# Attention, matrix products and a routed layer in one kernel: where the first two chunks are normalised, and which banks two hash products use

## The chip, the cores and the metric

The kernel runs as one program on one core of a Trainium2 chip. The metric is device microseconds (us) of one execution, from three runs: 702.88 us median, 701.33 to 703.13. The profile shown here is one more execution of the same program, with its own time of 702.02 us.

## The reference

Three layers follow each other, all in float32. Only the order of the arithmetic matters here.

```python
# 1. attention with hash buckets (B=2, H=8, S=768, D=64)
q_bits = (einsum('bhsd,dk->bhsk', q, proj) > 0)      # 6 bits, the same for k
mask   = q_bucket[:, :, :, None] == k_bucket[:, :, None, :]
scores = where(mask, (1 / sqrt(64)) * q @ k.T, -1e9)
scores = scores - max(scores)
attn   = exp(scores) / (sum(exp(scores)) + 1e-9)
x      = attn @ v                                    # as (1536, 512)
# 2. x = ((x @ w1) * (x @ w2)) @ w3 @ w_out
# 3. one of 8 experts per token
logits = x @ w_gate + modality_bias[modality_id]
e      = argmax(logits)
out    = softmax(logits)[e] * (relu(x @ w1[e]) @ w2[e])
```

## The kernel before

**Attention in units.** A pair is two heads side by side in the 128 partitions; there are 8 pairs. A pair has 12 units in the first stage (6 blocks of 128 queries times 2 heads) and 12 in the second (2 halves of 384 queries times 6 blocks of 128 keys). A loop over `i` (the unit number, 0 to 107) writes one step of each stage after the other, by hand; nothing reorders them. In unit i the first stage works on unit i and the second on unit i-9.

- `stage_1` (line 316): TensorE multiplies one block of queries by all keys (tile `m`, two banks, line 326), and VectorE takes the maximum of each row (`TENSOR_REDUCE nm<-m`, line 333). After six units GpSimd prepares the maxima (lines 337 to 340), `stage_f` transposes them (`f`, line 344), ScalarE copies them out (`rT`, line 346), and a DMA puts them into two extra rows of the query tile, so that the second stage gets them subtracted for nothing.
- `stage_2` (line 354): TensorE computes the scores (`s`, line 361), ScalarE takes the exponential (`pt<-s`, line 362), and the block is added to the running sum (`acc`, line 368), on GpSimd, and in some units on VectorE. `m` and `s` share one ring of two buffers (`ps("s")`, four banks in all), so a late maximum or a late exponential holds up TensorE.
- `stage_a` (line 371): TensorE multiplies by the values (`a`, line 376).

**Work between the units.** `fill` takes pieces of weights from a queue: three VectorE operations (lines 493, 494, 483) rebuild a weight from 64-bit storage, until unit 85. From unit 86 on (`SWITCH`) the pieces are loaded again (`st<-wfd`) and split into a high part (ScalarE, line 474) and a low part (`w<-st,w`, VectorE, line 475), 16 of them, for the second layer. The w3-times-w_out product (`w`, line 553) fills TensorE up to unit 85.

**Normalisation.** The attention output of a batch lies unnormalised in `xT`, as 4 slabs `hp` of 128 rows. A chunk is 256 tokens; there are six. `load_r(ch)` (line 577) loads the reciprocals of the sums, spread over the partitions, into `rb`. `norm_x(ch, hp, part)` (line 583) has three parts: part 0 multiplies by `rb` and adds a correction `nw` (mean of the values, for rows whose sum is zero), part 1 copies the result to a float32r tile on ScalarE (`x<-xT`, line 594), part 2 writes the remainder on VectorE (line 596). `norm_step` (line 598) runs part 0 of one slab, part 1 of the slab before and part 2 of the one before that.

- Chunk 0: `load_r` in unit 88, `norm_step` in units 90 to 95. Its part 0 is `nw` on VectorE (line 590), the product on GpSimd (line 591) and the sum on VectorE (line 592).
- Chunk 1: `load_r` in unit 98, part 0 in units 101 to 104, all three operations on VectorE.
- From chunk 2 on, in the second layer, product and sum are on GpSimd.

**After it.** From unit 95 on `moe_half` (line 620) issues the first products of the second layer (`ab`, line 627) between the units; the first one needs all four slabs of chunk 0. From about 327 us on the second layer, the routing and the experts run.

**The start.** `hash_z` (line 239) computes the hash products of the pairs, `hash_bits` (line 251) turns them into bits on VectorE (`bt<-z`, line 258). For the second pair, which has nothing but the first pair ahead of it, the two halves are computed in units 1 and 2 into the banks with the tags `m` and `w`, and turned into bits in units 6 and 7. `stage_f` uses the bank `m` as well, in unit 6.

Of the kernel before, what the change touches and what calls it, by code (L numbers as in the profile page):

```python
# [13 lines left out]
ALU = mybir.AluOpType  # L14
# [4 lines left out]
B, H, S, D = 2, 8, 768, 64  # L19
NT, DM, DF, E = 1536, 512, 1024, 8  # L20
P = 128
HP = H // 2
# [9 lines left out]
CH = 256  # L32
# [6 lines left out]
SWITCH = 86  # L39
# [15 lines left out]
NSTEP = 4  # L55
PATTERN = (1, 1, 0, 1, 0)
HOOKS = (3, 24, 82)
RAWS = 4


def consts_array(proj):
# [95 lines left out]
def body(tc, qT, kT, vP, w1d, w2d, w3d, wod, mod, wgate, mbias, e1, e2, cst, out):  # L157
    nc = tc.nc
    PE, ACT, DVE, POOL, SP = nc.tensor, nc.scalar, nc.vector, nc.gpsimd, nc.sync
# [4 lines left out]
    def one(name, shape, dt=F32, at_top=False):  # L164
        n = 4
        for d in shape[1:]:
            n *= d
        rings[name] = Ring(mem, name, n, 1, at_top)
        return rings[name](shape, dt)

    def ring(name, words, n, at_top=False, below=None):
        return Ring(mem, name, 4 * words, n, at_top, below)
# [15 lines left out]
    def ps(tag, shape, name):  # L188
        return psum[0].tile(shape, F32, tag=tag, name=name, bufs=nbuf.get(tag, 1))
# [8 lines left out]
    mv = one("mv", [P, B, HP])  # L198
# [4 lines left out]
    wgp = one("wgp", [P, 8, 32])  # L203
    xT = {b: one(f"xT{b}", [P, HP, S + 1]) for b in range(B)}

    r_raw = ring("raw", S, 6, True)
    r_bt = ring("bt", S, 1, True)
    r_lo = ring("lo", S, 2, True)
    heads = {
        (nm, hd, i): one(f"{nm}{hd}{i}", [P, 2, S], F32R, True) for i in range(2) for nm in "qk" for hd in range(2)  # L210
    }
# [24 lines left out]
    def hash_half(pairs, half):  # L236
        hash_z(pairs, half)
        hash_bits(pairs, half)

    def hash_z(pairs, half, tag="m"):  # L240
        z = zs_t[half] = ps(tag, [P, HS], f"z{pairs[0]}{half}")
        for p in pairs:
            for j, nm in enumerate("qk"):
                r = 64 * (p % 2) + 32 * j
                PE.matmul(
                    z[r:r + 32, :], cs[:, 96 + 32 * j:128 + 32 * j], raw_t[p, nm][:, half * 384:half * 384 + 384],
                    start=True, stop=True, tile_position=(0, r),
                )

    def hash_bits(pairs, half):  # L250
        lo, hi = 64 * (pairs[0] % 2), 64 * (pairs[-1] % 2) + 64
        z = zs_t.pop(half)
        if half == 0:
            bt = r_bt([P, S], F32R)
            for p in pairs:
                bt_t[p] = bt
        bt = bt_t[pairs[0]]
        DVE.tensor_scalar(
            bt[lo:hi, half * HS:half * HS + HS], z[lo:hi, :], cs[lo:hi, 2:3], cs[lo:hi, 0:1], ALU.is_ge, ALU.mult)
# [173 lines left out]
    def piece_load(k):  # L433
        i = order[k]
        if k in raws:
            return
        if i < 8:
            src = wod[i * P:(i + 1) * P, :]
        elif i < 24:
            f, hf = divmod(i - 8, 2)  # L440
            src = w3d[f, :, hf * 4:hf * 4 + 4, :].rearrange("p g f -> p (g f)")
        else:
            m, j = divmod((i - 24) % 16, 8)
            c, hf = divmod(j, 2)
            src = ((w1d, w2d)[m] if i < 40 else wfd[m])[c * P:(c + 1) * P, hf * 512:hf * 512 + 512]
        if i < 40:
            raws[k] = r_cr([P, 1024])
            SP.dma_start(raws[k].bitcast(I64), src)
        else:
            raws[k] = r_st([P, 512])  # L450
            SP.dma_start(raws[k], src)
# [70 lines left out]
    def after(n, fn):  # L522
        todo_at.setdefault(slot[0] + n, []).append(fn)
# [47 lines left out]
                break  # L571


    rg, w34 = {}, []
    x_t, g_t, gf_t, lg_t, rb_t, xn_t = {}, {}, {}, {}, {}, {}

    def load_r(ch):
        rb_t[ch] = rg["rb"]([P, HP, CH])
        b, o = divmod(ch * CH, S)
        for j in range(2):  # L580
            SP.dma_start(rb_t[ch][64 * j:64 * j + 64], rd[b, j, :, o:o + CH].partition_broadcast(64))

    def norm_x(ch, hp, part):
        b, o = divmod(ch * CH, S)
        if part and ch not in x_t:
            x_t[ch] = rg["x"]([P, 2, HP, CH], F32R)
        x = xT[b][:, hp, o:o + CH]
        if part == 0:
            w = rg["nw"]([P, CH])
            DVE.tensor_scalar(w, rb_t[ch][:, hp, :], 0.0, mv[:, b, hp:hp + 1], ALU.is_lt, ALU.mult)  # L590
            (DVE if ch == 1 else POOL).tensor_mul(x, x, rb_t[ch][:, hp, :])
            (DVE if ch < 2 else POOL).tensor_add(x, x, w)
        elif part == 1:
            ACT.copy(x_t[ch][:, 0, hp, :], x)
        else:
            DVE.tensor_sub(x_t[ch][:, 1, hp, :], x, x_t[ch][:, 0, hp, :].bitcast(F32))

    def norm_step(ch, step):
        for hp, part in ((step - 2, 2), (step - 1, 1), (step, 0)):
            if 0 <= hp < HP:  # L600
                norm_x(ch, hp, part)

    TERMS = ((0, 0), (0, 1), (1, 0))
# [124 lines left out]
    for i in range(NU + LEAD + LAG + 2):  # L728
        slot[0] = i
        if i == SWITCH:  # L730
            assert done["n"] == 40 and done["w"] == len(w34q), done
            for r in (r_cr, r_T, r_ev, r_wT, r_w3, r_wo):
                r.close()
            w12 = [one(f"w{m}", [P, 2, 4, DF], F32R) for m in range(2)]
            r_st = ring("st", 512, 3)
            for m in (40, 41, 42):
                piece_load(m)
            for r in (r_raw, r_bt, r_lo):
                r.close()
            rg["x"] = ring("x", 2 * HP * CH, 1, True)  # L740
            rg["rb"] = ring("rb", HP * CH, 1, True)
            rg["nw"] = ring("nw", CH, 1, True)
            rg["gf"] = ring("gf", 4 * CH, 1, True)
            rg["asb"] = ring("asb", CH, 1, True)
        if i == 0:
# [8 lines left out]
        if i == 12:  # L754
            SP.dma_start(cs[:, 160:], cst[:, 160:])
            SP.dma_start(wgs[:, :, 0:E], wgate.rearrange("(c p) e -> p c e", p=P))
        if i == SWITCH + NSTEP - 2:
            load_r(0)
        if 0 <= i - SWITCH - NSTEP < HP + 2:
            norm_step(0, i - SWITCH - NSTEP)  # L760
        if i == 98:
            load_r(1)
        if 101 <= i < 101 + HP:
            norm_x(1, i - 101, 0)
        if i == NU - 12 + LEAD:
            for nm in "qk":
                for hd in range(2):
# [6 lines left out]
        p, ph = divmod(i, 12)  # L774
# [6 lines left out]
        if fi % 6 == 0 and 0 < fi <= NU and (i <= 6 or fi > 6):  # L781
            stage_f(*divmod(fi // 6 - 1, 2))
        if p == 0 and ph in (1, 2):
            hash_z([1], ph - 1, "mw"[ph - 1])
        elif p == 0 and ph in (6, 7):
            hash_bits([1], ph - 6)
        elif p % 2 == 1 and p + 1 < NPAIR and ph in (HASH, HASH + 1):
            hash_half([p + 1, p + 2], ph - HASH)
        for fn in todo_at.pop(i, []):
# [155 lines left out]
    for ch in range(NCH):  # L945
        if ch:
            g_t[ch] = rg["g"]([P, 2, 8, CH], F32R)
        for f in range(NEARLY if ch == 0 else 0, 8):
            if ch == 0:
                k = f - NEARLY  # L950
# [135 lines left out]
    r_eu = ring("eu", 2 * 4096, 2)  # L1086
    r_er = ring("er", 1024, RAWS)
    r_ex = ring("ex", 2 * 4 * G, 2)
# [29 lines left out]
    def more_loads(n=1):  # L1118
        for _ in range(n):
            if lq:  # L1120
                j, m, k = lq.pop(0)
                load_raw(j, m, k, eregs[j])
# [17 lines left out]

    more_loads(RAWS - PREA)

# [86 lines left out]
    held.clear()  # L1229
    more_loads(RAWS - PREL)  # L1230

# [231 lines left out]
```

## Time and profile before

| | |
|---|---|
| median of 3 runs | 702.88 us (701.33 to 703.13) |
| the profiled execution, time / span | 702.02 us / 700.2 us |
| TensorE matmul, busy | 662.9 us (95%) |
| VectorE, ScalarE, GpSimd, busy | 383.3, 315.1, 318.9 us (55%, 45%, 46%) |
| mean granted TensorE clock | 0.975 of full speed |
| DMA | 94.03 MB, 134 GB/s over the span |

PE is TensorE (PEld its weight loads), DVE VectorE, ACT ScalarE, POOL GpSimd, SP the engine that issues the DMAs. In the timeline a line is one group of like instructions that follow each other: start, summed duration, engine, line, what is written and read, and in square brackets how long the engine sat idle before it and what ended that wait. A granted clock of 1.00 is 2.4 GHz and 0.50 is 1.2 GHz. The span begins with the first instruction; some 2 us of the execution's time lie outside it.

### The profile page before, as it was taken

To read this page: it belongs to the slowest core of one execution; us is meant where nothing else is said; L and a number is where in the kernel's file an instruction comes from. 1 tells how busy PE (TensorE), PEld (TensorE's weight loads), DVE (VectorE), ACT (ScalarE), POOL (GpSimd) and SP (SyncE) were. 2 spreads that over 40 slices of the span, in tenths; PEclk is the share of its full clock that TensorE was granted. 3 is DMA by queue.
4 is the path that set the end of the run, shared out by engine and by line. 5 is a ranking of instruction groups with operands and counts; after the bars stand their busy time and mean duration, and the time that the engine had idled before them with its cause. 6 is when DMAs were issued, how large, how long until landed. Compare 5 with 4: busy or idle time off the path is not lost. (4 is left out here: it accounts for less than half of the span.)

```text
span 700.2 us, 10953 instructions
## 1 busy us (share of the span) xinstructions
PE 662.9 (95%) x4004; PEld 507.0 (72%) x4004; DVE 383.3 (55%) x613; ACT 315.1 (45%) x534; POOL 318.9 (46%) x316
## 2 busy tenths in 40 slices
PE   6888999999999998899999999999998999999995
PEld 2544665656565664567989898989887999899884
DVE  6897676658657657746451212121184765665550
ACT  7256554646545555353341212121213765565551
POOL 8499867677867677344351414050204132011110
PEclk9699999999999998799999999999999999999998
DMA  8757654363826442230401020100017887666530
GB/s 225 240 180 177 203 157 161 117 203 111 245 78 215 135 145 88 88 102 24 115 19 61 1 61 1 61 1 31 0 62 270 270 295 231 231 209 214 202 126 18
DMA packets 41691, 94.03 MB, mean 134 GB/s; under 512 B 6352, under 2 KB 12032, under 8 KB 41632
## 3 DMA queue, kind: packets, MB, share of 16 engines
q1 hardware_dynamic: 39552, 86.72, 39.2%
q0 software_dynamic: 2080, 6.56, 2.8%
q8 instruction: 33, 0.54, 0.3%
q14 instruction: 26, 0.21, 0.1%
HBM read 72.98 MB, written 12.94 MB: 123 GB/s over the span
## 5 line engine op out<-in xcount | busy, mean ns | idle before, releaser
L627 PEld LDWEIGHTS ab<-x,w 128*128 128x128 f32 x1152 | 139.9, 191 | 11.5 <-issue 4.4
L627 PE MATMUL ab<-x,w 128*128 128x256 f32 x1152 | 144.5, 285 | 1.5 <-ACT rT L346 0.9
L333 DVE TENSOR_REDUCE nm<-m 128x1 f32<-128x768 f32 x96 | 91.4, 955 | 73.6 <-PE m L326 73.1
L368 POOL TENSOR_TENSOR acc<-acc,pt 128x770 f32<-128x770 f32 x61 | 112.9, 1851 | 26.1 <-ACT pt L362 24.8
L362 ACT ACTIVATE pt<-s 128x768 f32<-128x768 f32 x96 | 77.9, 812 | 93.3 <-PE s L361 84.4
L361 PE MATMUL s<-q,k 128*128 128x384 f32 (+1 forms) x384 | 88.7, 355 | 8.7 <-DVE nm L333 7.1
L638 POOL TENSOR_TENSOR g<-gf,g 128x256 fp32r<-128x256 f32 x48 | 35.5, 739 | 127.8 <-ACT g L637 127.6
L361 PEld LDWEIGHTS s<-q,k 128*128 128x128 f32 (+1 forms) x384 | 70.9, 197 | 21.0 <-DVE nm L333 8.7
L376 PE MATMUL a<-pt,v 128*64 128x385 f32 x384 | 84.7, 521 | 0.0
L1130 DVE TENSOR_TENSOR eu<-er,eu 128x1024 fp32r<-128x1024 f32 x56 | 67.4, 1223 | 23.3 <-ACT eu L1129 22.4
L326 PEld LDWEIGHTS m<-k,q 78*128 78x128 f32 x192 | 30.9, 200 | 63.2 <-issue 20.1
L1318 POOL DMA_INDIRECT out<-o,sidx x13 | 14.1, 1088 | 124.6 <-ACT o L1317 107.9
L1292 PE MATMUL e1F<-ex,eu 128*128 128x256 f32 x576 | 70.3, 283 | 0.5 <-DVE ex L1258 0.3
L1292 PEld LDWEIGHTS e1F<-ex,eu 128*128 128x128 f32 x576 | 69.7, 190 | 1.4 <-DVE ex L1258 0.5
L636 DVE TENSOR_TENSOR gf<-asb,ab 128x256 f32<-128x256 f32 x48 | 20.2, 421 | 90.4 <-ACT asb L635 90.3
L1310 PE MATMUL e2F<-eu,h 128*128 128x512 f32 x288 | 68.8, 394 | 0.0
L326 PE MATMUL m<-k,q 78*128 78x384 f32 x192 | 61.8, 407 | 6.7 <-DVE nm L333 4.1
L1129 ACT CAST eu<-er 128x1024 fp32r<-128x1024 f32 x56 | 57.6, 1046 | 8.5 <-DMA er<-e 7.7
L1310 PEld LDWEIGHTS e2F<-eu,h 128*128 128x128 f32 x288 | 53.3, 188 | 11.1
L553 PE MATMUL w<-wo,w 128*128 128x512 f32 x192 | 58.2, 410 | 0.8 <-POOL w L475 0.8
L926 PE MATMUL x2p<-w,g 128*128 128x512 f32 x240 | 58.2, 397 | 0.0
L635 ACT COPY asb<-ab 128x256 f32<-128x256 f32 x48 | 17.9, 373 | 78.2 <-PE ab L627 78.2
(200 smaller groups left out, 790.5 us busy)
## 6 DMA issues: line engine op xcount, KB each, us to landing
er<-e SPq DMA_DIRECT2D x56, 512.0 KB
cr<-w3d SPq DMA_DIRECT2D x16, 512.0 KB
cr<-wod SPq DMA_DIRECT2D x8, 512.0 KB
cr<-w1d SPq DMA_DIRECT2D x8, 512.0 KB
wfd<-cT SPq DMA_DIRECT2D x16, 256.0 KB
cr<-w2d SPq DMA_DIRECT2D x8, 512.0 KB
st<-wfd SPq DMA_DIRECT2D x16, 256.0 KB
raw<-kT SPq DMA_DIRECT2D x8, 384.0 KB
```

What stands on the lines that cost most here:

```text
L326: PE.matmul(s[:, half, 0:HS], q[0:KROWS[hd], 0, qt * P:qt * P + P], k[0:KROWS[hd], 0, half * HS:half * HS + HS], start=True, stop=True,)
L333: DVE.tensor_reduce(nm[:, 3 * hd + qt % 3:3 * hd + qt % 3 + 1], s[:, :, 0:HS], AX.XY, ALU.max, negate=True)
L361: PE.matmul(s[:, hd, 0:HS], k[0:n, i, c * P:c * P + P], q[0:n, i, cl], start=(i == 0), stop=(i == 1))
L362: ACT.activation(pts[j % 4][:, :, 0:HS], s[:, :, 0:HS], AF.Exp, scale=SCALE)
L368: (DVE if on_dve else POOL).tensor_add(acc, pts[(j - 1) % 4] if c == 1 else acc, pts[j % 4])
L376: PE.matmul(a_t[p, half][64 * hd:64 * hd + 64, :], v[:, c, 64 * hd:64 * hd + 64], pts[j % 4][:, hd, :], start=(c == 0), stop=(c == QT - 1) ...
L553: PE.matmul(w34p[f], w3_t[f][:, st, g, :], wo[:, mv, g, :], start=(g == 0 and k == 0), stop=(g == 7 and k == 2))
L627: PE.matmul(ab[:, j, :], w12[j][:, st, c, fs], x[:, mv, c, :], start=(c == 0 and i == 0), stop=(c == 3 and i == 2))
L926: PE.matmul(st["ps"], g_t[ch][:, a, f, i * P:i * P + P], w34[b][:, f, :], start=(f == 0 and k == 0), stop=(f == 7 and k == 2),)
L1130: DVE.tensor_sub(t[:, 1, sl], raw, t[:, 0, sl].bitcast(F32))
L1292: PE.matmul(o[f], w[:, st, c, fs], x[:, mv, c, :], start=(c == 0 and i == 0), stop=(c == 3 and i == 2))
L1310: PE.matmul(o, h[:, st, f, sl], w[:, mv, f, :], start=(f == 0 and k == 0), stop=(f == 7 and k == 2))
```

## The change

Chunk 0 and chunk 1 get their reciprocals in units 74 and 90 (before: 88 and 98), and the twelve operations of part 0 of each are written one per unit, from unit 78 and from unit 94, all on VectorE, behind the unit's maximum and the queue's first operation. `norm_step` leaves part 0 out for these two chunks; parts 1 and 2 stay where they were. The rings `rb` and `nw` are taken at the start, and the ring `lo` loses its second buffer. The second pair's hash products go to the banks `u` and `w`, and the second half's bits are taken in unit 8.

```diff
+NORM = (74, 90)
...
+    rg = {"rb": ring("rb", HP * CH, 1, True), "nw": ring("nw", CH, 1, True)}
     r_raw = ring("raw", S, 6, True)
     r_bt = ring("bt", S, 1, True)
-    r_lo = ring("lo", S, 2, True)
+    r_lo = ring("lo", S, 1, True)
...
             DVE.tensor_scalar(w, rb_t[ch][:, hp, :], 0.0, mv[:, b, hp:hp + 1], ALU.is_lt, ALU.mult)
-            (DVE if ch == 1 else POOL).tensor_mul(x, x, rb_t[ch][:, hp, :])
-            (DVE if ch < 2 else POOL).tensor_add(x, x, w)
+            POOL.tensor_mul(x, x, rb_t[ch][:, hp, :])
+            POOL.tensor_add(x, x, w)
...
+    def norm_0(ch, hp, s):
+        b, o = divmod(ch * CH, S)
+        x = xT[b][:, hp, o:o + CH]
+        if s == 0:
+            DVE.tensor_mul(x, x, rb_t[ch][:, hp, :])
+        elif s == 1:
+            nw_t[ch, hp] = rg["nw"]([P, CH])
+            DVE.tensor_scalar(nw_t[ch, hp], rb_t[ch][:, hp, :], 0.0, mv[:, b, hp:hp + 1], ALU.is_lt, ALU.mult)
+        else:
+            DVE.tensor_add(x, x, nw_t.pop((ch, hp)))
+
     def norm_step(ch, step):
         for hp, part in ((step - 2, 2), (step - 1, 1), (step, 0)):
-            if 0 <= hp < HP:
+            if 0 <= hp < HP and (part or ch >= len(NORM)):
                 norm_x(ch, hp, part)
...
-        if i == SWITCH + NSTEP - 2:
-            load_r(0)
         if 0 <= i - SWITCH - NSTEP < HP + 2:
             norm_step(0, i - SWITCH - NSTEP)
-        if i == 98:
-            load_r(1)
-        if 101 <= i < 101 + HP:
-            norm_x(1, i - 101, 0)
+        for ch, at in enumerate(NORM):
+            if i == at and ch == 0:
+                load_r(0)
+            if i == at + 4:
+                for k in range(12):
+                    after(k, lambda ch=ch, k=k: norm_0(ch, k // 3, k % 3))
+            if i == at + 16 and ch + 1 < len(NORM):
+                load_r(ch + 1)
...
         if p == 0 and ph in (1, 2):
-            hash_z([1], ph - 1, "mw"[ph - 1])
-        elif p == 0 and ph in (6, 7):
-            hash_bits([1], ph - 6)
+            hash_z([1], ph - 1, "uw"[ph - 1])
+        elif p == 0 and ph in (6, 8):
+            hash_bits([1], ph // 2 - 3)
```

VectorE's order before, from the maximum of unit 89 to that of unit 92 (`m_2_1`, `m_3_0`, `m_3_1` and `m_4_0` are units 89 to 92):

```order
L333 TENSOR_REDUCE nm_2328<-m_2_1_2435 128x1
L368 TENSOR_TENSOR acc_2430<-acc_2430,pt_20_89 128x770
L475 TENSOR_TENSOR w_215_2368<-st_2370,w_215_2368 128x512
L590 TENSOR_SCALAR nw_2457<-rb_2414,mv_73 128x256
L592 TENSOR_TENSOR xT_10_79<-xT_10_79,nw_2457 128x256
L333 TENSOR_REDUCE nm_2464<-m_3_0_2461 128x1
L475 TENSOR_TENSOR w_216_2369<-st_2372,w_216_2369 128x512
L590 TENSOR_SCALAR nw_2481<-rb_2414,mv_73 128x256
L592 TENSOR_TENSOR xT_10_79<-xT_10_79,nw_2481 128x256
L333 TENSOR_REDUCE nm_2464<-m_3_1_2485 128x1
```

The same place in the changed kernel, whose line numbers are 2 higher here (lines 604, 607 and 609 are the three operations of `norm_0`):

```order
L335 TENSOR_REDUCE nm_2339<-m_2_1_2450 128x1
L609 TENSOR_TENSOR xT_10_79<-xT_10_79,nw_2434 128x256
L370 TENSOR_TENSOR acc_2445<-acc_2445,pt_20_89 128x770
L477 TENSOR_TENSOR w_219_2382<-st_2384,w_219_2382 128x512
L335 TENSOR_REDUCE nm_2479<-m_3_0_2476 128x1
L477 TENSOR_TENSOR w_220_2383<-st_2386,w_220_2383 128x512
L335 TENSOR_REDUCE nm_2479<-m_3_1_2496 128x1
L477 TENSOR_TENSOR w_219_2382<-st_2388,w_219_2382 128x512
L477 TENSOR_TENSOR w_220_2383<-st_2471,w_220_2383 128x512
L598 TENSOR_TENSOR x_2494<-xT_10_79,x_2494 128x256
L335 TENSOR_REDUCE nm_2479<-m_4_0_2525 128x1
```

Each pair of `nw` and sum has gone from in front of the maxima of units 90 to 93; what is left of part 0 there is the last sum of chunk 0, right behind the maximum of unit 89.

GpSimd's order before, at the same place:

```order
L368 TENSOR_TENSOR acc_2430<-pt_22_91,pt_23_92 128x770
L337 TENSOR_SCALAR nm_2328<-nm_2328 128x6
L338 TENSOR_TENSOR nm_2328<-nm_2328 128x6
L339 CAST nm_2328<-nm_2328 128x2x3
L340 TENSOR_TENSOR nm_2328<-nm_2328 128x2x3
L591 TENSOR_TENSOR xT_10_79<-xT_10_79,rb_2414 128x256
L368 TENSOR_TENSOR acc_2430<-acc_2430,pt_21_90 128x770
```

Of the four products (line 591) the first stands here, and the other three follow behind this block sum and the next two; in the changed kernel all four are gone from GpSimd, and nothing takes their place there.

VectorE's order in the changed kernel, units 84 to 88, is the pattern of all twelve units from 78 on:

```order
L335 TENSOR_REDUCE nm_2339<-m_0_0_2336 128x1
L604 TENSOR_TENSOR xT_10_79<-xT_10_79,rb_2059 128x256
L335 TENSOR_REDUCE nm_2339<-m_0_1_2356 128x1
L607 TENSOR_SCALAR nw_2366<-rb_2059,mv_73 128x256
L335 TENSOR_REDUCE nm_2339<-m_1_0_2390 128x1
L609 TENSOR_TENSOR xT_10_79<-xT_10_79,nw_2366 128x256
L335 TENSOR_REDUCE nm_2339<-m_1_1_2411 128x1
```

Between each two maxima there now stands one operation of part 0, where before nothing stood in these units.

VectorE's order in the changed kernel at the start, units 6 to 9 (`z_166` and `z_174` are the two halves of the second pair's hash product, `m_3_0` to `m_4_1` units 6 to 9):

```order
L335 TENSOR_REDUCE nm_218<-m_3_0_215 128x1
L260 TENSOR_SCALAR bt_226<-z_166,cs_71 64x384
L335 TENSOR_REDUCE nm_218<-m_3_1_229 128x1
L335 TENSOR_REDUCE nm_218<-m_4_0_237 128x1
L260 TENSOR_SCALAR bt_226<-z_174,cs_71 64x384
L335 TENSOR_REDUCE nm_218<-m_4_1_248 128x1
```

The second half's bits have moved behind the maximum of unit 8; the order of TensorE is the same in both kernels, but its transposition `f` of unit 6 now writes a bank that no bits are read from.

## Rows read from the trace of the kernel before

**Rows 1.** Timeline of PE, units 89 to 95: start, duration, then idle time before.
```profile
266.18 0.61 PE L326 MATMUL m<-k,q 128*128 128x384 f32 x2
...
268.22 0.62 PE L326 MATMUL m<-k,q 78*128 78x384 f32 x2
...
274.06 0.97 PE L361 MATMUL s<-q,k 78*128 78x384 f32 x4 [2.83 <-DVE nm L333]
...
276.00 1.01 PE L326 MATMUL m<-k,q 78*128 78x384 f32 x2
...
279.70 1.01 PE L326 MATMUL m<-k,q 128*128 128x384 f32 x2
283.57 1.65 PE L361 MATMUL s<-q,k 78*128 78x384 f32 x4 [2.87 <-DVE nm L333]
...
289.88 0.62 PE L326 MATMUL m<-k,q 128*128 128x384 f32 x2
...
291.94 1.69 PE L627 MATMUL ab<-x,w 128*128 128x256 f32 x12
```

**Rows 2.** Windows: busy PE, PEld, DVE, ACT, POOL; granted clock, DMA share, GB/s.
```profile
235.00:268.00 33.00, 32.66 (x179) 19.81 (x177) 19.22 (x25) 17.16 (x27) 22.27 (x16) 1.00 0.49 142
...
274.00:276.00 2.00, 1.85 (x9) 0.85 (x9) 1.90 (x5) 0.87 (x2) 0.00 (x0) 0.91 0.14 48
...
288.00:290.00 2.00, 2.00 (x8) 0.83 (x8) 1.16 (x2) 0.85 (x2) 0.09 (x1) 0.68 0.67 224
```

**Rows 3.** Timeline of DVE, units 89 to 95.
```profile
266.83 0.96 DVE L333 TENSOR_REDUCE nm<-m 128x1 f32<-128x768 f32 x1 [1.09 <-PE m L326]
268.51 0.96 DVE L368 TENSOR_TENSOR acc<-acc,pt 128x770 f32<-128x770 f32 x1 [0.72 <-POOL nm L337]
269.38 0.69 DVE L475 TENSOR_TENSOR w<-st,w 128x512 fp32r<-128x512 f32 x1
...
271.13 2.01 DVE L592 TENSOR_TENSOR xT<-xT,nw 128x256 f32<-128x256 f32 x1 [0.80 <-POOL xT L591]
273.06 0.94 DVE L333 TENSOR_REDUCE nm<-m 128x1 f32<-128x768 f32 x1
...
274.98 0.43 DVE L592 TENSOR_TENSOR xT<-xT,nw 128x256 f32<-128x256 f32 x1
...
284.03 0.42 DVE L596 TENSOR_TENSOR x<-xT,x 128x256 fp32r<-128x256 f32 x1
...
292.55 0.94 DVE L333 TENSOR_REDUCE nm<-m 128x1 f32<-128x768 f32 x1
```

**Rows 4.** Timeline of POOL, units 83 to 91.
```profile
252.09 1.83 POOL L293 TENSOR_TENSOR k<-raw,k 64x768 fp32r<-64x768 f32 x1
...
258.73 5.66 POOL L368 TENSOR_TENSOR acc<-acc,pt 128x770 f32<-128x770 f32 x3
266.44 1.86 POOL L368 TENSOR_TENSOR acc<-pt,pt 128x770 f32<-128x770 f32 x1 [2.05 <-ACT pt L362]
...
270.36 0.73 POOL L591 TENSOR_TENSOR xT<-xT,rb 128x256 f32<-128x256 f32 x1
271.05 1.81 POOL L368 TENSOR_TENSOR acc<-acc,pt 128x770 f32<-128x770 f32 x1
```

**Rows 5.** Timeline of PE at the start, units 6 to 9.
```profile
19.57 0.37 PE L344 MATMUL f<-ident,nm 128*12 128x128 f32 x1 [1.84 <-DVE bt L258]
...
23.43 1.65 PE L361 MATMUL s<-q,k 78*128 78x384 f32 x4 [0.70 <-DVE nm L333]
```

**Rows 6.** Timeline of SP's DMA issues, the same stretch.
```profile
14.14 2.18 SPq L448 DMA_DIRECT2D cr<-wod  x3
20.26 1.57 SPq L349 DMA_DIRECT2D q<-rT  x2
```

**Rows 7.** Timeline of PE, a wait in an earlier stretch of the attention.
```profile
152.11 0.94 PE L361 MATMUL s<-q,k 78*128 78x384 f32 x4 [1.02 <-DMA q<-rT]
```

**Rows 8.** The page, part 2: granted clock in 40 slices of 17.5 us, in tenths.
```profile
PEclk9699999999999998799999999999999999999998
```

More of the change, by code (lines that the diff above doesn't have):

```diff
@@ L571, in w34_step @@
                 break
-    rg, w34 = {}, []
-    x_t, g_t, gf_t, lg_t, rb_t, xn_t = {}, {}, {}, {}, {}, {}
+    w34 = []
+    x_t, g_t, gf_t, lg_t, rb_t, nw_t = {}, {}, {}, {}, {}, {}
     def load_r(ch):
@@ L740, in body @@
             rg["x"] = ring("x", 2 * HP * CH, 1, True)
-            rg["rb"] = ring("rb", HP * CH, 1, True)
-            rg["nw"] = ring("nw", CH, 1, True)
             rg["gf"] = ring("gf", 4 * CH, 1, True)
```

## Prediction

> **What bounds the kernel now.** First the page: TensorE is busy for 95% of the span, so an edit can only give back time in which TensorE waits or runs slowly. The clock row [rows 8] shows where it runs slowly: slice 1, counted from 0 (17.5 to 35 us), and slices 15 and 16 (262 to 297 us), which is where chunk 0 is normalised. The timeline of TensorE [rows 1] shows the second place. Unit 89 takes 2.04 us (266.18 to 268.22). Then TensorE stands still twice, for 2.83 us before 274.06 and for 2.87 us before 283.57, each time for a maximum of VectorE, and the five units from 90 on take 21.66 us (268.22 to 289.88) where five of unit 89's length would take 10.2: 11.5 us are lost here. A part of that is the clock. A granted clock of 0.91 over 274 to 276 us is 0.36 us at half speed, so it fell at about 275.6; 0.68 over 288 to 290 is 1.28 us at half speed, so it rose again at about 289.3 [rows 2]. For 13.6 us, behind the first standstill, TensorE ran at 1.2 GHz.
>
> Why the maxima come late is in the timelines of VectorE and GpSimd [rows 3, 4]. The product of unit 90 ends at 268.84 (268.22 + 0.62), but its maximum starts at 273.06. Ahead of it stands the sum of chunk 0's first slab, which first waits 0.80 us for GpSimd's product (270.36 + 0.73) and then takes 2.01 us, though the same operation takes 0.43 at 274.98. GpSimd's block sum runs from 271.05 to 272.86, and the sum ends at 273.14, 0.28 us later: it seems to stand until GpSimd's operation is over. Maxima, which read PSUM, keep their 0.95 us. So an elementwise VectorE operation from SBUF to SBUF pays up to 1.8 us when it meets a GpSimd operation.
>
> **The change, part by part.**
>
> *Units 90 to 95.* Taken away: four products on GpSimd, four `nw` and four sums on VectorE, and the handover between them. New start of the chain: the maximum of unit 89 ends at 267.79 (266.83 + 0.96) [rows 3]; the last sum of chunk 0 waits for the block sum until 268.30 (266.44 + 1.86) [rows 4] and ends at 268.73 with its 0.43; the block sum on VectorE takes 0.96, the first weight split 0.69: 270.4, and 270.8 with 0.4 us from units 78 to 89 (below). So the maximum of unit 90 starts 2.3 us earlier. From there to the end of the maximum of unit 95 VectorE has, by the order, 6 maxima of 0.95, 7 weight splits of 0.69, 4 remainders of 0.42 and one product of chunk 1, at the sum's 0.43: 5.7 + 4.8 + 1.7 + 0.4 = 12.6 us. GpSimd has four block sums of 1.85 there. None in the way is one bound (12.6), each in the way for its whole length the other (12.6 + 7.4 = 20.0). I take the half, 3.7, since a block sum often falls beside a maximum, which does not wait for it: 16.3 us, end at 287.1. Before, it ended at 293.5 (292.55 + 0.94): **6.4 us** gained, bounds 2.7 and 10.0. With 3.3 us a unit the chain stays the limit, TensorE at full clock needing 2.04; the sum therefore supposes that the clock stays up, with many short waits of TensorE in place of two long ones. A wait of 1.02 us at 152 us [rows 7] lies in slice 8, whose clock stayed at 9 [rows 8]. What is late next is the weight splits.
>
> *Units 78 to 89.* Added: twelve operations of at most 0.43 us, 5.2 us of VectorE, which is busy for 19.22 of 33 us there, while TensorE is busy for 32.66 [rows 2]. The work that hides them is TensorE's; a maximum has to wait. GpSimd is the danger: it works without a pause from before 252.09 to 264.39 (258.73 + 5.66) and again from 266.44 [rows 4], and about seven of the twelve meet it. On average one waits half of 1.85 and takes 0.43, 1.35 us, in a unit that leaves 1.1 us (2.04 - 0.95) or more. I take 0.4 us for the one in unit 83, which comes just behind the start at 252.09 and has two more operations behind it ahead of the next maximum. Bounds: 0, and 8.3 if all seven wait fully and overrun by 1.2 us each. It is in the 270.8 above. GpSimd in its turn is pushed back by some 3 us and has 2.05 us of slack before 266.44; the rest is within the bounds.
>
> *Chunk 1 in units 94 to 105.* The same twelve operations as before, spread instead of packed into four units. One of them is counted above. The others lie beside the second layer's products, 1.69 us more for TensorE in each unit from 291.94 on [rows 1]: nothing; without that cover 11 x 0.43 = 4.7 us.
>
> *The moved loads.* Two DMAs each, earlier by 14 and 8 units, so nothing waits for them. They pass weight loads in SP's queue; some 1.6 us of issue (the pair at 20.26 took 1.57 [rows 6]) against three loads kept ahead: nothing, at worst 1.6 us each. The single `lo` buffer makes ScalarE's copy for the second pair wait for the first pair's DMA; ScalarE's next duty is the copy behind `f` at 19.57 [rows 5], so nothing, at worst what the start gains.
>
> *The start.* `f` of unit 6 stood 1.84 us behind the bits that VectorE still had to read from its bank [rows 5]. That wait goes. What is late next: the scores of 23.43 need the DMA that is issued at 20.26, behind three loads of 512 KB issued from 14.14 on [rows 6], and if those are still under way, an earlier issue lands little earlier. Bounds 0 and 1.84; nearer to the first, because of these loads: **0.6 us**.
>
> Sum against the profiled execution: 702.0 - 6.4 - 0.6 = 695.0. The median of the runs is 0.86 us above that execution, so the forecast for the median is **695.9 us**. The bounds of the terms give 691.1 (10.0 and 1.84 gained) and 700.2 (2.7 and 0).
>
> [...]
>
> **The rivals.**
>
> 1. *The clock falls all the same.* If one maximum waits for a whole block sum behind two splits and a remainder (1.85 + 0.7 = 2.55 us), the new stretch has a standstill like the old ones, behind which the clock fell. Suppose it falls at 280 and stays down for 13.6 us. Three units then take 3.70 (276.00 to 279.70 [rows 1]) instead of 3.3, 1.2 us, and 6.6 us of the units behind them run at half speed, 3.3 us: 695.9 + 4.5 = 700.4. For: GpSimd's sums and VectorE's splits both start when an exponential is done. Against: only one of several chances has to go wrong, but each by luck of a few tenths. Chance 0.12.
> 2. *VectorE hardly waits for GpSimd.* Then 10.0 are gained: 702.9 - 10.0 - 0.6 = 692.3. For: operations that fall between block sums keep their 0.43. Against: four block sums of 1.85 in some 16 us. Chance 0.13.
> 3. *The wait only moves.* The splits meet every block sum, as the sums did: 2.7 gained, nothing at the start, 700.2. For: the splits stand right where the sums stood. Against: four handovers to GpSimd are gone in any case. Chance 0.10.
> 4. *Slower: units 78 to 89 become what the sums were in units 90 to 93.* Each operation there meets a block sum or a `k` of 1.8 us; seven overruns of 1.2 us make 8.3, and if the clock falls once as in [rows 2], 13.6 us at half speed cost up to 6.8 more. Against 7.0 gained this is 702.9 + 8.1 = 711. It decides from the point where TensorE's new waits before unit 90 pass 7.0 us. For: GpSimd has no pause there. Against: VectorE is idle for 13.8 of 33 us, and one operation per unit leaves it time. Chance 0.05. The Trainium skill (SBUF — State Buffer, "SBUF: two separate sides") has the later of the two blocked for the other's whole length, which is this rival's price for each; 2.01 us against 1.81 agrees.
>
> **How the numbers follow.** The forecast's own case, 693.5 to 698.5, has 0.60. A measurement tells some 0.3% (2.1 us) from no change, here 700.8. Faster: 0.60 + 0.13, most of rival 3 and half of rival 1, together 0.83. Within 0.3%: the rest of these two, 0.12 with a slower start or lost cover. Slower: 0.05. The range goes from 692.0, which takes in the second rival, to 700.8, which takes in the third and most of the first.
>
> **What would show it.** Right: TensorE's two waits of 2.8 us gone, the granted clock at 1.00 from 262 to 297 us, the first `ab` some 6 us earlier, VectorE's maximum of unit 90 at about 270, remainders and splits of up to 2 us still there, and `f` without its wait for the bits. Wrong: a clock below 1.00 between 250 and 297 us, waits of over a microsecond for a maximum in units 78 to 95, or a first `ab` that is less than 3 us earlier.

## The result, and the profile after

| | before | changed |
|---|---|---|
| median of the runs | 703.0 us (701.33 to 703.14, 4 runs) | 696.02 us (691.33 to 696.57, 4 runs) |
| ratio | | 0.9887 (95% interval 0.9859 to 0.9916) |
| the profiled execution, time / span | 702.02 / 700.2 us | 696.55 / 694.7 us |
| mean granted TensorE clock | 0.975 | 0.983 |

The changed kernel is 7 us faster, as forecast (695.9 us). Ten runs in two series (the second, below, has a median of 694.35 us) have a middle of 694.6 us. The forecast's terms did not all come out, though, and errors of both signs offset each other.

First the clock row of the page, to be read against [rows 8], then TensorE's timeline of units 90 to 95, to be read against [rows 1].

```profile
PEclk9699999999999999999999999999999999999999
```

```profile
271.13 0.62 PE L328 MATMUL m<-k,q 78*128 78x384 f32 x2
...
273.41 0.62 PE L328 MATMUL m<-k,q 128*128 128x384 f32 x2 [0.16 <-ACT pt L364]
...
276.75 0.62 PE L328 MATMUL m<-k,q 78*128 78x384 f32 x2 [1.07 <-DVE nm L335]
...
280.17 0.96 PE L363 MATMUL s<-q,k 78*128 78x384 f32 x4 [0.50 <-DVE nm L335]
...
286.88 1.69 PE L640 MATMUL ab<-x,w 128*128 128x256 f32 x12
```

The product of unit 90 stands at 271.13, the first `ab` 15.75 us behind it; before it was 23.72 us (268.22 to 291.94 [rows 1]). So 7.97 us went here. Waits of TensorE were 5.86 us before (0.16 + 2.83 + 2.87) and are 2.05 (three of 0.16, 1.07 and 0.50): 3.8 us. The other 4.2 us are the products, which no longer run at the lower clock: slices 15 and 16 of the clock row are at 9, where they were at 8 and 7.

VectorE and GpSimd in the same stretch, to be read against [rows 3, 4] (the rows from 253 to 255 us belong to unit 83):

```profile
254.29 0.68 DVE L495 TENSOR_SCALAR u<-cr 128x512 int32<-128x512 int32 x1
254.89 2.07 DVE L609 TENSOR_TENSOR xT<-xT,nw 128x256 f32<-128x256 f32 x1
...
271.42 0.96 DVE L370 TENSOR_TENSOR acc<-acc,pt 128x770 f32<-128x770 f32 x1
...
272.90 0.95 DVE L335 TENSOR_REDUCE nm<-m 128x1 f32<-128x768 f32 x1
273.90 1.93 DVE L477 TENSOR_TENSOR w<-st,w 128x512 fp32r<-128x512 f32 x1
...
276.62 2.29 DVE L477 TENSOR_TENSOR w<-st,w 128x512 fp32r<-128x512 f32 x2
...
280.04 1.48 DVE L477 TENSOR_TENSOR w<-st,w 128x512 fp32r<-128x512 f32 x1
...
287.71 0.94 DVE L335 TENSOR_REDUCE nm<-m 128x1 f32<-128x768 f32 x1
```

```profile
253.03 1.85 POOL L370 TENSOR_TENSOR acc<-pt,pt 128x770 f32<-128x770 f32 x1 [3.63 <-DMA wfd<-cT]
254.84 1.83 POOL L295 TENSOR_TENSOR k<-raw,k 64x768 fp32r<-64x768 f32 x1
...
271.67 0.77 POOL L340 TENSOR_TENSOR nm<-nm 128x6 f32<-128x6 f32 x1
...
273.44 1.84 POOL L370 TENSOR_TENSOR acc<-acc,pt 128x770 f32<-128x770 f32 x1
275.94 1.82 POOL L370 TENSOR_TENSOR acc<-acc,pt 128x770 f32<-128x770 f32 x1 [0.66 <-ACT pt L364]
279.14 1.83 POOL L370 TENSOR_TENSOR acc<-acc,pt 128x770 f32<-128x770 f32 x1 [1.38 <-ACT pt L364]
```

Weight splits of 0.69 us [rows 3] take 1.93, 2.29 for two and 1.48 us; the first and the last end 0.55 us behind the end of a block sum (275.28 and 280.97). The chain of VectorE, from the maximum of unit 90 to the end of that of unit 95, runs from 272.90 to 288.65 (287.71 + 0.94), 15.75 us.

The windows, for [rows 2], and for the start and the place of [rows 7]:

```profile
18.00:20.00 2.00, 1.10 (x4) 0.31 (x2) 1.94 (x3) 0.00 (x0) 1.15 (x1) 0.71 0.98 276
...
32.00:34.00 2.00, 2.00 (x11) 1.15 (x9) 1.59 (x3) 0.99 (x2) 1.92 (x3) 0.87 0.71 238
...
155.00:160.00 5.00, 5.00 (x19) 3.35 (x16) 0.96 (x1) 2.25 (x4) 0.13 (x1) 0.66 0.04 14
235.00:268.00 33.00, 32.56 (x177) 20.11 (x176) 27.34 (x36) 18.12 (x28) 23.53 (x20) 1.00 0.46 141
274.00:276.00 2.00, 1.68 (x10) 0.76 (x8) 2.00 (x2) 1.44 (x4) 1.34 (x2) 1.00 0.77 232
```

VectorE is busy for 27.34 us from 235 to 268, where it was for 19.22, and TensorE's busy time in that window is only 0.1 us less. At the start, 0.71 over 18 to 20 us is 1.16 us at half speed, so the clock fell at 18.8, and by the 0.87 it rose at 32.5; before, worked out alike (0.55 over 16 to 18 us and 0.53 over 28 to 30), it fell at 16.2 and rose at 29.9.

TensorE's timeline at the start and at 152 us, for [rows 5, 7]:

```profile
17.43 0.28 PE L346 MATMUL f<-ident,nm 128*12 128x128 f32 x1
...
23.20 1.62 PE L363 MATMUL s<-q,k 78*128 78x384 f32 x4 [1.86 <-DMA q<-rT]
...
153.67 0.94 PE L363 MATMUL s<-q,k 78*128 78x384 f32 x4 [1.94 <-DMA q<-rT]
```

`f` has lost its wait, but the scores it serves now stand 1.86 us for the DMA of `rT`, and start only 0.23 us earlier. Behind the wait of 153.67 the granted clock fell to 1.2 GHz (0.66 over 155 to 160 us), which it did not do before behind 1.02 us.

The span's 5.5 us, place by place, from the same product in both traces: +0.65 us up to a product at 56 us (55.83 to 56.48), +2.1 between there and unit 78 (234.43 to 237.17; the wait of 153.67 and the low clock behind it make +2.45, and 0.3 is regained just ahead of unit 78), +0.17 in units 78 to 89 (268.22 to 271.13), -7.97 up to the first `ab`, and the last -0.4 behind it.

### The profile page after: what moved, and what is told of

Same layout as the page of the kernel before. It is cut to its first block, busy times and chain, and to the rows that moved or that the text cites. A ratio compares the mean times of both kernels' runs of the same rounds, so it can differ in the third digit from the quotient of the medians.

```text
span 694.7 us, 10961 instructions
## 1 busy us (share of the span) xinstructions
PE 660.1 (95%) x4004; PEld 505.6 (73%) x4004; DVE 381.8 (55%) x617; ACT 315.4 (45%) x534; POOL 316.4 (46%) x312
## 5 line engine op out<-in xcount | busy, mean ns | idle before, releaser
L328 PEld LDWEIGHTS m<-k,q 78*128 78x128 f32 x192 | 29.9, 194 | 65.0 <-issue 18.5
```

The source lines that it names most:

```text
L328: PE.matmul(s[:, half, 0:HS], q[0:KROWS[hd], 0, qt * P:qt * P + P], k[0:KROWS[hd], 0, half * HS:half * HS + HS], start=True, stop=True,)
```

## Experiments

Each is timed against the kernel before in its own series; those medians were 701.3 to 703.0 us.

**Which part gains.** The changed kernel without the hash part of the change:

```diff
-            hash_z([1], ph - 1, "uw"[ph - 1])
-        elif p == 0 and ph in (6, 8):
-            hash_bits([1], ph // 2 - 3)
+            hash_z([1], ph - 1, "mw"[ph - 1])
+        elif p == 0 and ph in (6, 7):
+            hash_bits([1], ph - 6)
```

> The changed kernel with the second pair's hash products back in the banks of before. What the hash part does at the start was forecast as 0.6 us gained; the trace of the changed kernel shows its products 0.65 us later than before from the second pair on. Theory A (the hash part loses at the start, because the clock falls later there and its low stretch then lies over fuller units): products of units 15 to 60 at the places of before, within 0.1 us, f again with a wait of 1.84 us, time 0.65 us below the changed kernel's, about 695.4 us. Theory B (the forecast): products 0.6 us later than in the changed kernel, about 696.6 us. Both theories: the first ab 16 us behind the product of unit 90, as in the changed kernel.

Measured 695.48 us (694.53 to 697.03), ratio 0.9888 (0.9864 to 0.9912): the whole gain, within what the two can be told apart. The first `ab` came 15.98 us behind unit 90. The clock at the start went against theory A: it stayed at 0.50 until about 38 us (before: 29.9), and the product at 56 us came 1.86 us later than before, with the start's old order. So the 0.65 us of the changed kernel's trace can't be put down to the hash part.

The other half, in the kernel before:

```diff
-            hash_z([1], ph - 1, "mw"[ph - 1])
-        elif p == 0 and ph in (6, 7):
-            hash_bits([1], ph - 6)
+            hash_z([1], ph - 1, "uw"[ph - 1])
+        elif p == 0 and ph in (6, 8):
+            hash_bits([1], ph // 2 - 3)
```

> The kernel before with the hash part of the change alone. Theory A (it loses at the start): 0.65 us slower than before, about 703.6 us; f without a wait at about 17.4 us, the first scores 1.9 us behind the DMA of rT, the low clock from about 18.8 to 32.6 us. Theory B (the forecast): 0.6 us faster, 702.4 us. A third possibility is that the shift of the start, of either sign, decides whether the DMA of rT that is waited for at 152 us is late enough for the clock to fall there: then the time moves by 2 us more, and the trace shows it by a granted clock below 1.00 between 150 and 165 us.

Measured 702.8 us (700.34 to 705.78, 12 runs), ratio 0.9995 (0.9975 to 1.0014): no difference, between both theories. `f` lost its wait, and the first scores stood 1.71 us for `rT`; the low clock lasted from 17.8 to 34.8 us, longer than theory A had it. The third possibility did not occur: no wait and no fall at 152 us.

This trace also shows how far units 90 to 95 vary where their code is that of before:

```profile
268.52 0.62 PE L326 MATMUL m<-k,q 78*128 78x384 f32 x2
...
294.59 1.69 PE L627 MATMUL ab<-x,w 128*128 128x256 f32 x12
```

Here they take 26.07 us, 2.35 more than in the kernel before, because the clock stayed low for 20.5 us (0.77 over 255 to 300 us) and not for 13.7 (0.85).

**Place or crowding.** The kernel before with the product moved in place:

```diff
-            (DVE if ch == 1 else POOL).tensor_mul(x, x, rb_t[ch][:, hp, :])
+            (DVE if ch < 2 else POOL).tensor_mul(x, x, rb_t[ch][:, hp, :])
```

> The kernel before with chunk 0's product on VectorE instead of GpSimd, where it stood: no handover between the two engines, but all twelve operations still in units 90 to 93. Theory A (most of the gain comes from taking the operations out of these units): VectorE still has 1.2 us of them in each of four units ahead of its maximum, in all 15.8 us from the maximum of unit 90 to the end of that of unit 95, and 3.7 of waiting for block sums, 19.5 us against 20.4 before and 15.8 in the changed kernel; the first ab 2 to 3 us earlier than before, about 700.5 us, and standstills of TensorE of 1 to 2 us still there. Theory B (the handover was the cost): the first ab 6 to 8 us earlier, about 695.5 us, clock at 1.00 throughout.

Measured 701.51 us (699.3 to 704.27), ratio 0.9981 (0.9961 to 1.0001). TensorE and VectorE in its trace:

```profile
268.13 0.62 PE L326 MATMUL m<-k,q 78*128 78x384 f32 x2
...
273.46 1.65 PE L361 MATMUL s<-q,k 78*128 78x384 f32 x4 [2.33 <-DVE nm L333]
...
282.98 1.65 PE L361 MATMUL s<-q,k 78*128 78x384 f32 x4 [1.74 <-DVE nm L333]
...
290.65 1.69 PE L627 MATMUL ab<-x,w 128*128 128x256 f32 x12
```

```profile
270.62 1.92 DVE L592 TENSOR_TENSOR xT<-xT,nw 128x256 f32<-128x256 f32 x1
272.46 0.94 DVE L333 TENSOR_REDUCE nm<-m 128x1 f32<-128x768 f32 x1
```

Theory A: 22.52 us from unit 90 to `ab`, 1.2 less than before, less even than its 2 to 3; its chain of maxima takes 19.75 us (272.46 to 292.21), as worked out (19.5). So the handover between the engines was the small part. The sum still meets a block sum right ahead of the maximum, the standstill is 2.33 us, and the clock falls behind it.

In the changed kernel, the twelve operations of chunk 0 packed again, but ahead of that stretch, in units 86 to 89 (chunk 1 packed, as in the experiment on it below):

```diff
-                    after(k, lambda ch=ch, k=k: norm_0(ch, k // 3, k % 3))
+                    after(8 + k // 3, lambda ch=ch, k=k: norm_0(ch, k // 3, k % 3))
```

> The changed kernel with chunk 0's twelve VectorE operations packed three to a unit, as before, but in units 86 to 89, where VectorE has no weight splits, instead of spread over units 78 to 89; chunk 1 packed as before. The change did two things to them, spread them and took them out of units 90 to 93; this does the second alone. Theory A (the place is what counts): the maximum's 0.95 and 1.2 us of the three go into 2.04 us of TensorE per unit, with some waits behind block sums; the product of unit 90 comes up to 2 us later against that of unit 78, the first ab 15.7 us behind it as in the changed kernel, clock 1.00 throughout; 694.5 to 696.5 us. Theory B (it is the crowding in one unit that costs): a maximum two blocked operations late, TensorE standing for over 2 us before unit 90 and the clock falling behind that as in the kernel before; 699 to 702 us.

Measured 700.37 us (695.18 to 703.18, 10 runs), ratio 0.9954 (0.9928 to 0.998). VectorE and TensorE:

```profile
262.30 1.92 DVE L607 TENSOR_SCALAR nw<-rb,mv 128x256 f32<-128x256 f32 x1
264.25 2.02 DVE L609 TENSOR_TENSOR xT<-xT,nw 128x256 f32<-128x256 f32 x1
...
278.59 2.60 DVE L477 TENSOR_TENSOR w<-st,w 128x512 fp32r<-128x512 f32 x2 [0.23 <-ACT w L476]
281.11 2.03 DVE L598 TENSOR_TENSOR x<-xT,x 128x256 fp32r<-128x256 f32 x1
```

```profile
267.19 0.62 PE L328 MATMUL m<-k,q 78*128 78x384 f32 x2 [1.58 <-DVE nm L335]
...
272.78 0.62 PE L328 MATMUL m<-k,q 78*128 78x384 f32 x2 [1.31 <-DVE nm L335]
...
284.06 1.65 PE L363 MATMUL s<-q,k 78*128 78x384 f32 x4 [2.76 <-DVE nm L335]
...
292.43 1.69 PE L640 MATMUL ab<-x,w 128*128 128x256 f32 x12
```

Crowding is what costs: two of the three operations ahead of one maximum each stand behind a GpSimd sum (3.9 us in place of 0.8). The time is theory B's, but only a part of the loss lies where theory B put it. From unit 78 to unit 90 this profile takes 36.83 us where the changed kernel takes 33.96; the waits are 1.58 and 1.31 us, and the clock stays up. The other 3.9 us are lost in units 90 to 95 (19.65 us to `ab`), where nothing was added: the block sums come at other moments, two splits and a remainder stand behind them, TensorE stands for 2.76 us, and there the clock falls. A spread of 8 us over the runs suggests that this does not happen in each execution.

**What is left in units 90 to 95.** The changed kernel without three block sums:

```diff
-        if c:
+        if c and not (81 <= j < 84):
             acc = acc_t[p, half]
```

> The changed kernel without GpSimd's three block sums of units 90 to 92 (blocks 3 to 5 of one half of one pair are left out of the sum of the exponentials). Theory A (what is left of the stretch's cost is VectorE standing behind GpSimd): the weight splits that took 1.93, 2.29 for two and 1.48 us go to 0.69 each, 2.9 us less on VectorE's chain, and the first ab comes 13.5 to 14.3 us behind the product of unit 90, not 15.75, where TensorE's own work is the limit; 694.5 us against 696.0. Theory B (VectorE's own work is the chain): 15.75 stays within 0.3 us, and 696.0.

Measured 693.23 us (692.19 to 695.77), ratio 0.9874 (0.9835 to 0.9912); in the trace:

```profile
271.66 0.69 DVE L477 TENSOR_TENSOR w<-st,w 128x512 fp32r<-128x512 f32 x1
...
274.09 1.29 DVE L477 TENSOR_TENSOR w<-st,w 128x512 fp32r<-128x512 f32 x2 [0.86 <-ACT w L476]
```

```profile
268.90 0.62 PE L328 MATMUL m<-k,q 78*128 78x384 f32 x2
...
276.98 0.94 PE L363 MATMUL s<-q,k 78*128 78x384 f32 x4 [0.71 <-DMA q<-rT]
...
283.88 1.68 PE L640 MATMUL ab<-x,w 128*128 128x256 f32 x12
```

Between the two theories in the trace; by the times alone this kernel can't be told from the changed one (694.35 us in the same series). The splits take 0.69 us as soon as GpSimd is idle, so the GpSimd sum was what they stood behind: theory A's mechanism. But only 0.77 us of the 2.9 reaches `ab` (14.98 us): other waits take their place, the longest 0.71 us for the DMA of `rT`.

**Chunk 1.**

```diff
-            if i == at + 4:
+            if i == at + 4 and ch == 0:
...
-            if i == at + 16 and ch + 1 < len(NORM):
-                load_r(ch + 1)
+        if i == 98:
+            load_r(1)
+        if 101 <= i < 101 + HP:
+            for s in (1, 0, 2):
+                norm_0(1, i - 101, s)
```

> The changed kernel with chunk 1's twelve operations packed into units 101 to 104 and its load in unit 98, as before; chunk 0 stays spread. Theory A (the forecast: chunk 1's operations lie beside the second layer's products either way): time of the changed kernel within 0.5 us, about 696.0 us, and no wait of TensorE for a maximum in units 101 to 104. Theory B (spreading chunk 1 gave part of the gain): 1 to 3 us slower, 697 to 699 us, with waits for maxima in units 101 to 104. One operation of chunk 1 less lies in units 94 and 95, so the first ab may come some 0.5 to 1.5 us earlier (it waited 1.37 us for a block sum in the changed kernel).

Measured 694.16 us (693.19 to 695.86), ratio 0.9873 (0.9842 to 0.9904). Theory A in that nothing is lost; the time is below its range, but 0.2 us from the changed kernel's second series. Its sign, no wait for a maximum in units 101 to 104, can't tell the theories apart, since the first stage ends with unit 95 and no maximum is left there. What tells is TensorE: sums of chunk 1 take 1.97 us beside a GpSimd operation, and the units remain 3.11 us apart. The first `ab` came 15.74 us behind unit 90, not earlier: with the product gone, the next split met the block sum instead (1.50 us).

**The start, and the wait at 152 us.** The three weight loads taken from ahead of `rT`, and each pair's values two units later:

```diff
-        if i == 5:
-            for m in range(3):
-                piece_load(m)
...
             stage_f(*divmod(fi // 6 - 1, 2))
+        if i == 6:
+            for m in range(3):
+                piece_load(m)
...
-            if j % 12 == 3 and j // 12 + 1 < NPAIR:
+            if j % 12 == 5 and j // 12 + 1 < NPAIR:
```

> The changed kernel with loads taken from ahead of the DMA of rT: the first three weight loads of 512 KB issue behind the first rT in unit 6 (before it, in unit 5), and each pair's values (384 KB) load two units later, behind the second rT. Theory A (rT lands late because these loads stand ahead of it): the first scores, at 23.2 us with a wait of 1.86 us, start 1 to 1.5 us earlier, part of it given back by the low clock there; the wait of 0 to 1.94 us at 152 us, seen in some kernels and not in others, is gone in the profile. 694.0 to 695.5 us against 696.0. Theory B (rT is not late because of its neighbours, or the scores wait for something else next): the same time within 0.5 us, and the first scores wait for rT or a maximum as long as before.

Measured 693.92 us (693.64 to 694.98), ratio 0.9874 (0.9843 to 0.9906): just below theory A's range, but 0.4 us from the changed kernel's own second series (below), and its trace is half theory B. The scores start at 21.44 us without a wait, and then the second pair's first product stands for rows that queue behind the same three loads:

```profile
32.31 0.98 PE L328 MATMUL m<-k,q 78*128 78x384 f32 x2 [2.64 <-DMA q<-bt]
```

The other way, `rT` on ScalarE's queue, in `stage_f`:

```diff
-            SP.dma_start(
+            ACT.dma_start(
                 head_t[p, hd, "q"][r:r + 2, 0, half * HS:half * HS + HS].bitcast(F32),
```

> The changed kernel with the DMAs of rT issued by ScalarE, which also makes rT, instead of SP. Theory A (what delays rT is the queue): the first scores lose their wait of 1.86 us, and what ScalarE pays is two issues of some 0.7 us per six units (a pair takes 1.57 us on SP), which the exponentials behind them feel: TensorE waits for pt for up to 0.5 us in 16 places. Between 693 and 702 us; 697 as the middle. Theory B (the DMA engines are full, whichever queue): the wait of 1.86 us stays within 0.4 us.

Measured 701.02 us (698.06 to 702.91), ratio 0.9971 (0.9946 to 0.9995). The first scores waited 2.11 us: theory B, another queue doesn't help. All 16 DMA engines are busy while they wait (share 1.01 to 1.04 from 20 to 24 us). What made it slow was unforeseen. In units 90 to 92, GpSimd, VectorE, TensorE:

```profile
276.10 1.85 POOL L370 TENSOR_TENSOR acc<-acc,pt 128x770 f32<-128x770 f32 x1 [1.52 <-ACT pt L364]
278.38 1.82 POOL L370 TENSOR_TENSOR acc<-acc,pt 128x770 f32<-128x770 f32 x1 [0.42 <-ACT pt L364]
```

```profile
276.50 4.25 DVE L477 TENSOR_TENSOR w<-st,w 128x512 fp32r<-128x512 f32 x2 [0.50 <-ACT w L476]
```

```profile
270.45 0.62 PE L328 MATMUL m<-k,q 78*128 78x384 f32 x2
...
282.00 1.65 PE L363 MATMUL s<-q,k 78*128 78x384 f32 x4 [3.09 <-DVE nm L335]
...
291.98 1.70 PE L640 MATMUL ab<-x,w 128*128 128x256 f32 x12
```

ScalarE's two DMA issues (1.27 us) delay one exponential; two block sums now follow each other, two splits stand behind both, the maximum is late, TensorE stands for 3.09 us and its clock falls: 21.53 us to `ab`, 5.8 more than in the changed kernel. This is the first rival of the prediction, in a kernel that differs by 1.27 us of ScalarE's time per six units.

The changed kernel again:

> The changed kernel once more, beside the others of this series. If the waits for the DMA of rT at 152 us, and the clock that falls behind it, differ from execution to execution, its times spread from 691 to 697 us as in its first four, around 695.5, and its profile may show no wait at 152 us; if they belong to the kernel, the wait of about 1.9 us is there again and the times stay at 695.5 to 696.6.

Measured 694.35 us (692.84 to 695.99), ratio 0.9879 (0.985 to 0.9909). Its profile (693.68 us) has no wait and a clock of 1.00 at 152 us, and 15.72 us from unit 90 to `ab`; at the start its clock stays low for 17.1 us, where the first profile of the same kernel has 13.7. Of the thirteen profiles here only two show that wait, those of the kernels before and after first shown; what makes `rT` late in them was not found.

Loads taken apart, one in unit 5, one behind `rT`, one behind the second pair's rows; the values two units later, chunk 1 packed:

```diff
-            for m in range(3):
-                piece_load(m)
+            piece_load(0)
...
+        if i == 6:
+            piece_load(1)
...
                 d_qlo(1)
+                piece_load(2)
```

> The changed kernel with chunk 1 packed as before, each pair's values loaded two units later, and the first three weight loads of 512 KB taken apart: one in unit 5, as now, one behind the first DMA of rT in unit 6, one behind the second pair's rows in unit 8. Theory A (the loads ahead of rT, and then those ahead of the second pair's rows, are what the start waits for): no wait of the first scores for rT above 0.5 us (1.26 to 1.86 in the changed kernel) and none of the second pair's first product for its rows (2.64 us when all three loads stood behind rT); 1.5 us below the changed kernel's last median, 692.8 us, since part is lost to the low clock. Theory B (one wait takes the place of the other): 694 to 694.5 us, with a wait of over 1 us in the profile between 20 and 36 us.

Measured 691.85 us (690.5 to 692.36), ratio 0.9841 (0.9815 to 0.9866): theory A and a microsecond more, and the lowest median of all versions, 2.5 us below the changed kernel's second series, whose lowest run is 692.84 (the first series has one run of 691.33). What the split loads and the later values give apart was not measured. The first scores and the second pair's first product have no wait:

```profile
21.44 1.65 PE L363 MATMUL s<-q,k 78*128 78x384 f32 x4
...
29.60 1.01 PE L328 MATMUL m<-k,q 78*128 78x384 f32 x2
```

The same kernel without the hash part:

```diff
-            hash_z([1], ph - 1, "uw"[ph - 1])
-        elif p == 0 and ph in (6, 8):
...
+            hash_z([1], ph - 1, "mw"[ph - 1])
+        elif p == 0 and ph in (6, 7):
...
```

> The kernel with the three first weight loads taken apart and the values later, but with the second pair's hash products in the banks of before. Theory A (the hash part's gain at the start was real and hidden behind the loads, so that it shows once these are out of the way): f waits 1.84 us again, the first scores start some 9 us behind the product of unit 5 instead of 6.74, and the time is 1.5 to 2.5 us above the kernel that has both, 693.4 to 694.4 us against 691.85. Theory B (the loads alone made that gain): 691.4 to 692.4 us.

Measured 692.62 us (691.59 to 692.68), ratio 0.9859 (0.9804 to 0.9913). `f` waits 1.84 us and the scores start at 24.04 us, 9.20 us behind the product of unit 5 (14.84). From that product to a transposition at some 117 us (`pt<-ident,wT`) it takes 103.17 us against 101.48 with the hash part: 1.7 us in the trace, theory A's lower end, and the mean granted clock over 14 to 42 us is 0.70 in both, so the clock does not account for it. By the ratios it is 1.3 us, with intervals that overlap; the time alone does not settle it.

## Why the prediction was right or wrong

**Units 90 to 95** (forecast -6.4, bounds -2.7 and -10.0, with units 78 to 89 in it): right in mechanism, too small by 1.4. Measured -7.97 + 0.17 = -7.8. Counted as the prediction did, on the clock of before (2.91 us off the changed kernel's times, since unit 90's product is that much later), the maximum of unit 90 starts at 269.99, forecast 270.8, and the chain ends at 285.74, forecast 287.1. The chain's length was nearly right, 15.75 against 16.3, but partly by luck: the operations that met a GpSimd operation (splits of 1.93, 2.29 and 1.48 us and chunk 1's product, 1.80) stand for 4.4 us in all, where half of the block sums' length, 3.7, had been put, and VectorE's own work takes 11.3 us, not 12.6, mostly because records that follow each other overlap by some 0.1 us. The chain's start had been put 0.8 us too late. That the clock would stay up with short waits in place of long ones is shown: the longest left is 1.07 us. This is just over the microsecond that had been named as a sign of being wrong, and the clock did not fall behind it. In the trace's own time the first `ab` is 5.1 us earlier (291.94 to 286.88), not some 6, since 2.9 us are lost ahead of unit 90. The 1.4 us are no more than what this stretch varies by without the change (23.72 and 26.07 us).

**Units 78 to 89** (forecast +0.4 at the chain's start): +0.17. The operation of unit 83 did meet GpSimd (2.07 us beside the `k` of 254.84), as named; TensorE lost its 0.17 us behind it. Seven of the twelve took longer than alone, as forecast, by 5.1 us in all, nearly all of it hidden behind TensorE's work. One operation per unit is what keeps this cheap: three per unit cost 2.9 us before unit 90.

**Chunk 1 and the moved loads** (0): right as far as is seen. The packed chunk 1 costs nothing either, and no operation of part 0 waits for its reciprocals; ScalarE's copy into the single `lo` buffer is not held up (15.78 us at the start, 15.53 before).

**The start** (forecast -0.6, bounds 0 and -1.84): the step that failed, in that no gain shows, which was the bound that the prediction leaned to. The wait before `f` went, and what was named as late next, the DMA behind three loads, took 1.86 of it. From unit 5's product to the transposition at some 117 us, the three profiles with the old banks and the old loads take 102.28 (the kernel before), 103.21 and 103.64 us, six with the new banks 102.39 to 103.02 (the changed kernel 102.69). So it gained nothing that shows among executions that differ by more than a microsecond, depending on where the clock rises again (29.9 to 38 us). Beside profiles of the same mean clock over 14 to 42 us, the new banks lose 0.1 to 0.4 us (clock 0.76, three profiles against one), and gain 0.4 (0.70, two against one) and 0.6 (0.63, one against one): too few to tell. The 1.84 us become a gain of 1.7 once the loads stand elsewhere.

**What the sum did not have:** 2.1 us in one execution, from the wait at 153.67 and the clock behind it. With the start's +0.65 it hides the 1.4 us that the first term was short, so that the median met the forecast in part by luck: the profiled execution's 696.55 is 1.5 above its forecast of 695.0, and the changed kernel's second profile, without that wait, is 1.3 below it (693.68). The prediction's row of 1.02 us at 152 us was read as harmless, which it was in that execution; it was not a stable row.

**The rivals.** The second (VectorE hardly waits, 692.3) is excluded by the split rows. The third (the wait only moves, 700.2) did not happen: 7.8, not 2.7 us. The fourth did not happen with one operation per unit. The first did not happen in the changed kernel, but it did in two neighbours, at 5.8 and 3.9 us where 4.5 was worked out; the parts were others, though, standstills of 3.09 and 2.76 us and a clock that stayed low for some 10 and 7 us, not 13.6 (0.89 and 0.92 over 255 to 300 us).

## What to carry to other kernels

When a maximum or another small result releases TensorE, count the operations that stand ahead of it on its engine, and ask how many may each meet a long GpSimd operation: one costs little, two or three together cost a standstill, and the lower clock behind it can double the price (here 4.2 us beside 3.8). Spread such operations one to a unit over an earlier stretch in which the engine has room, and then read the new stretch again, because a shift of a microsecond elsewhere can line them up again. A wait that is removed is worth only as much as what is late next allows: look for that, and move it too. Where the DMA engines are all busy, move the large loads and not the queue.

## What the runs showed of the hardware

- An elementwise VectorE operation from SBUF to SBUF stands until a running GpSimd operation ends, also where it has one tensor input: `nw` took 1.92 us in place of 0.34 beside a block sum. Maxima, which read PSUM, kept 0.95 us, and so did the three operations that rebuild weights, one operand of which lies in PSUM (`ps("u")` in the kernel): 0.68 us at 254.29, beside the block sum of 253.03, and 0.68 to 0.70 us wherever else they met one. It goes the other way too: GpSimd's operation on the maxima takes 0.77 us at 271.67 in the changed kernel, beside VectorE's block sum of 271.42, where it otherwise takes 0.20.
- Behind standstills of 2.33 to 3.09 us for a maximum the granted clock fell to 1.2 GHz, and behind 1.07, 1.31 and 1.58 us in units 88 to 92 it did not. How long it stayed low differs: 13.7 us in the kernel before, 20.5 in the one with the hash part alone, some 10 and 7 in two others. Behind 1.94 us at 153.67 it fell for 3.4 us only. At the start it stayed low for 13.7 us in the first profiles of the kernel before and the changed one, for 17.1 in the second of the changed one, and for 20.5 in others.
- A small DMA that is issued while all 16 DMA engines are busy waits on either queue: `rT` kept the scores for 1.86 us behind loads on its own queue and for 2.11 us on ScalarE's, with a DMA share of 1.00 to 1.04 from 20 to 24 us in both; with the loads taken apart the share is 0.42 from 20 to 21 us, and the scores do not wait.
